# Weights in 4 KB rows with block-diagonal stationaries, and mode-mix groups pinned to iterations, in an attention plus spectral-mix kernel

## The chip, the cores and the metric

The kernel runs on one core of one Trainium2 chip. The metric is device time in microseconds. The kernel before takes 456.05 us, the median of three runs (455.77 to 456.72). A core has a matrix engine (PE; its weight loads are listed apart as PEld), a vector engine (DVE), a scalar engine (ACT), a general engine (POOL), a queue engine (SP), and 16 DMA engines which all of them share.

## The reference

Two stages follow one another. The first is linear attention with a learned feature map, for 8 batches, 8 heads, 576 tokens and head size 64:

```python
proj = einsum('bhsd,df->bhsf', x, w_phi)            # 64 -> 128 features
proj = proj - max(abs(proj), axis=-1, keepdims=True)
phi  = concatenate([exp(proj), exp(-proj)], -1)     # 256 features
kv = einsum('bhsf,bhsd->bhfd', phi(k), v);  z = sum(phi(k), axis=2)
out = einsum('bhsf,bhfd->bhsd', phi(q), kv) / (einsum('bhsf,bhf->bhs', phi(q), z) + 1e-6)
```

The heads side by side make x of 8 x 576 x 512. The second stage mixes it in the frequency domain and adds a channel mix:

```python
X = rfft(x, axis=1)                                  # the first 64 modes are used
Yr = einsum('bmd,mde->bme', Xr, w_r) - einsum('bmd,mde->bme', Xi, w_i)
Yi = einsum('bmd,mde->bme', Xr, w_i) + einsum('bmd,mde->bme', Xi, w_r)
y = irfft(Y, n=576, axis=1)                          # other modes are zero
u = x + y;  result = u + relu(u @ w_ch)
```

Every mode has its own 512 x 512 matrices w_r and w_i in float32. Together they are 134.2 MB, by far the most that the kernel reads; q, k and v are 9.4 MB each, and the result is 9.4 MB.

## The kernel before, in words

**Attention.** 32 items are worked through in a software pipeline of 34 iterations (`for n in range(N + 2)`, L555). Items 0 to 7 are one head for two batches, first head 0 and then head 1 (the first quarter of the 512 channels together, 64 each). Items 8 to 31 are two heads (128 channels, called a quarter g = 1, 2 or 3) of one batch. In iteration n, item n gets its features, item n-1 its products, and item n-2 its forward transform (`x_mm`, L344), which multiplies a token block by a cosine and sine matrix (`CF4`) and leaves the spectrum of 64 modes. `psx` holds it, and ACT copies it into XT0 or XT1. Each engine's order is the order in which the program is written (manual schedule).

**XT.** A tile XT0 or XT1 has a row per channel (128) and 80 columns of 64 modes. Columns 16 to 31 and 48 to 63 hold the spectrum for 8 batches in two parts each; columns 0 to 15, 32 to 47 and 64 to 79 are zero. A stationary of 32 columns that begins at column 0, 16, 32 or 48 puts a mode's 16 rows of result into the upper or the lower half of a 32-row strip, so that two modes share a strip and zeros are added for the other one. XT1 serves head 0 and g = 1 and 3; XT0 serves head 1 and g = 2.

**Mode mix.** The weights come in 32 groups, k = 0 to 31. Groups 0 to 7 are 16 modes for 64 channels each (four DMAs of 1 MB read, the two halves of a tile apart, L167). Groups 8 to 31 are 8 modes for 128 channels: one DMA for w_r and one for w_i (L162), each 2 MB of float32 read and 1 MB of bfloat16 written, as 1,024 rows of 512 numbers (2 KB read, 1 KB written). `mode_mm(k)` multiplies a group (L403, L416), and `mode_sum(k)` adds it to `Yacc` on DVE. The tiles of a group lie in a pool with three buffers (`bufs=3`), so a group k+3 can be loaded once group k has been multiplied.

**What sets the order.** At most one `mode_mm` stands in an iteration, as the last of PE's work there; it runs in the first iteration that is at least `after[k] + 2` and is written up to k = 21. The others follow attention, each with some pieces of the channel mix (`pieces(plan[k])`: transposes of x, their product with w_ch) and every second one with `by_batch`. In an iteration, POOL's order is: loads of q and k (odd n only, `load_qk`, for iterations n+5 and n+6), then `weights(k_in)` while `k_in < k_out + 3`, and then `vscale` (L270, L275), which scales v by the feature factors and whose result `vaug` PE needs for `kv_mm` (L286) one iteration later. All loads that change the type (weights, q, k, w_ch) are issued by POOL on one queue (q0). The built program gives these transfers eight completion counters in turn, so each waits on POOL until the one eight before it has landed, and what stands behind it on POOL waits too. Loads of v and stores go through SP (q1).

Of the kernel before, what the change touches and what calls it, by code (L numbers as in the profile page):

```python
# [21 lines left out]
NCH = 5  # L22
# [4 lines left out]
def kernel(  # L27
# [11 lines left out]
    nc = tc.nc  # L39
# [14 lines left out]
    xs_all = pers.tile([128, B_ * NCH, DMODEL], BF16, name="xs_all")  # L54
# [8 lines left out]
    CF4 = const.tile([128, NCH, 4, 64], BF16, name="CF4")  # L63
# [3 lines left out]
    XTs = [XT0, XT1]  # L67
# [88 lines left out]
    def weights(k):  # L156
        g, gi = groups[k]
        wt = {}
        for ri, w in ((0, moe_w_r), (1, moe_w_i)):
            t = pw.tile([128, 8, DMODEL], BF16, name=f"w{'ri'[ri]}", tag=f"w{ri}")  # L160
            if gi >= 0:
                nc.gpsimd.dma_start(  # L162
                    t, w[8 * gi:8 * gi + 8, g * 128:(g + 1) * 128, :].rearrange("m p e -> p m e"))
            else:
                for x in range(2):
                    mx = 16 * (-1 - gi) + 8 * x
                    nc.gpsimd.dma_start(  # L167
                        t[64 * x:64 * x + 64],
                        w[mx:mx + 8, g * 64:(g + 1) * 64, :].rearrange("m p e -> p m e"))
            wt[ri] = t  # L170
        W[k] = wt
# [172 lines left out]
    def x_mm(st):  # L344
        psx = psum.tile([128, 2, 4, 64], F32, name="psx", tag="tx", bufs=1)
        XT = XTs[st["xt"]][:, 16:80, :].rearrange("p (x y b) m -> p x y b m", x=2, y=4)
        if "bs" in st:

            h = st["h"]
            for i, b in enumerate(st["bs"]):  # L350
                for c in range(NCH):
                    for x in range(2):
                        nc.tensor.matmul(
                            psx[64 * x:64 * x + 64, i, :, :],
                            lhsT=xs_all[:, b * NCH + c, h * 64:(h + 1) * 64],
                            rhs=CF4[:, c, :, :],
                            start=(c == 0), stop=(c == NCH - 1),
                        )
        else:
            g = st["g"]  # L360
            for c in range(NCH):
                nc.tensor.matmul(
                    psx[:, 0, :, :],
                    lhsT=xs_all[:, st["b"] * NCH + c, g * 128:(g + 1) * 128],
                    rhs=CF4[:, c, :, :],
                    start=(c == 0), stop=(c == NCH - 1),
                )
        for i, b in enumerate(st["bs"] if "bs" in st else (st["b"],)):
            nc.scalar.copy(
                XT[:, :, 0:2, b, :],  # L370
                psx[:, i, :, :].rearrange("d (x y) m -> d x y m", x=2),
            )
# [17 lines left out]
    def mode_mm(k, tag="yr"):  # L390
        g, gi = groups[k]
        XT = XTs[1 - g if k < 8 else g % 2]
        wt = W.pop(k)
        if gi < 0:
            psY = psum.tile([128, 2, DMODEL], F32, name="psY2", tag="pC", bufs=1)
            for par in range(2):
                for ri in range(2):
                    for j in range(4):
                        for x in range(2):
                            r = slice(64 * x, 64 * x + 64)  # L400
                            m = 16 * (-1 - gi) + 8 * x + 2 * j + par
                            c0 = (16, 0, 48, 32)[2 * ri + par]
                            nc.tensor.matmul(  # L403
                                psY[32 * j:32 * j + 32, x, :],
                                lhsT=XT[r, c0:c0 + 32, m],
                                rhs=wt[ri][r, 2 * j + par, :],
                                start=(par == 0 and ri == 0), stop=(par == 1 and ri == 1),
                            )
            return psY
        psY = psum.tile([128, DMODEL], F32, name="psY", tag=tag, bufs=1)  # L410
        for ri in range(2):
            for par in range(2):
                for j in range(4):
                    m = 8 * gi + 2 * j + par
                    c0 = (16, 0, 48, 32)[2 * ri + par]
                    nc.tensor.matmul(  # L416
                        psY[32 * j:32 * j + 32, :],
                        lhsT=XT[:, c0:c0 + 32, m],
                        rhs=wt[ri][:, 2 * j + par, :],
                        start=(par == 0 and ri == 0), stop=(par == 1 and ri == 1),  # L420
                    )
        return psY

# [26 lines left out]
    def zeros(i):  # L450
        for z in (0, 32, 64):
            nc.vector.memset(XTs[i][:, z:z + 16, :], 0.0)

    def setup():

# [68 lines left out]

    psY = None
    k_in = k_out = 0
    K_IN_ATTN = 22
    pa_last_cm = None
    with tc.manual_schedule():
        load(S[0], "qk")  # L530
        setup()
        load(S[0], "v")
        load(S[1])
        zeros(1)
        casts(S[0], nc.vector)
        casts(S[1], nc.gpsimd, "q")
        load_qk(1)
        for t in AAs:
            nc.gpsimd.memset(t[:, 0, :, 1152:1216], 1.0)
        for t in e2s:  # L540
            nc.gpsimd.memset(t[64:128, :, NCH - 1:NCH], 1.0)
        casts(S[1], nc.gpsimd, "k")

        pa_first_cm.__exit__(None, None, None)
        pa_last_cm = tc.tile_pool(name="pa_last", bufs=1)
        pa_last = pa_last_cm.__enter__()
        qk2s[2] = qk_pair(pa_last, 2)
        for t in qk2s[2]:
            nc.gpsimd.memset(t[:, :, 9, :], 0.0)
        load_qk(2)  # L550
        weights(0)
        k_in = 1
        transp(S[0], "q")
        transp(S[0], "k")
        for n in range(N + 2):  # L555
            cur = S[n] if n < N else None
            prev = S[n - 1] if 0 <= n - 1 < N else None
            old = S[n - 2] if 0 <= n - 2 < N else None
            nxt = S[n + 1] if n + 1 < N else None
            if n + 2 < N:  # L560
                load(S[n + 2])
            if cur:
                feat_tok(cur, "k", "pB")
                feat_q(cur)
            if psY is not None:
                mode_sum(k_out, psY)
                psY = None
                k_out += 1
            if cur:
                rem_mm(cur)  # L570
                absmax(cur, "k")
                absmax(cur, "rem")
                exps(cur, "q")
            if nxt:
                transp(nxt, "q")
            if prev:
                kv_mm(prev)
                kv_cp(prev)
            if cur:
                ekq(cur, "k")  # L580
            if n < 4:
                vscale(cur)
            if n % 2 == 1 and 5 <= n < N - 5:
                load_qk((n + 5) // 2)
            while k_in < min(k_out + NW, 2 if n < 3 else 32):
                weights(k_in)
                k_in += 1
            if n in (1, 3):
                load_qk((n + 5) // 2)
            if n == 16:  # L590
                nc.gpsimd.dma_start(wchb, moe_w_ch.rearrange("(dc p) e -> p dc e", p=128))
            if cur and n >= 4:
                vscale(cur)
            if nxt:
                transp(nxt, "k")
            if cur:
                exps(cur, "k")
                exps(cur, "rem")
            if prev:
                num_mm(prev, 1)  # L600
                numer(prev, 0)
                num_mm(prev, 0)
                numer(prev, 1)
                numer(prev, 2)
            if old:
                x_mm(old)
            e = n - (N + 2 - N_EARLY)
            if e >= 0:
                sTe = flip_early(e)
            if cur:  # L610
                feat_tok(cur, "q", "pA")
                absmax(cur, "q")
                ekq(cur, "q")
            if n == 0:
                forward_matrix()
            if n == 2:
                zeros(0)
            if 10 <= n < 10 + NCH:
                inverse_matrix(n - 10)
            if e >= 0:  # L620
                times_w_early(e, sTe)
            if k_out < K_IN_ATTN and n >= after[k_out] + 2:
                psY = mode_mm(k_out)
    if psY is not None:
        mode_sum(k_out, psY)
# [157 lines left out]
    u0 = dict(bc=((0, 0), (0, 1)), half=False, late=False, tags=("T2", "T3"))  # L783

    with tc.manual_schedule():
        plan = {22: 3, 23: 3, 24: 2, 25: 2, 26: 2, 27: 1, 28: 2, 29: 1, 30: 1, 31: 0}
        while k_out < 32:
            k = k_out
            gi = groups[k][1]
# [97 lines left out]
```

## Time and profile before

The profiled execution has a span of 456.7 us, against the median of 456.05 us over the three runs and the highest, 456.72 us.

| what | before |
|---|---|
| PE busy, granted clock (mean) | 301.7 us (66%), 0.88 |
| DVE, ACT, POOL busy | 292.0 us, 261.8 us, 198.8 us |
| read from HBM, written to it | 163.64 MB, 9.44 MB |
| weights of groups 8 to 31 | 48 DMAs of 1,024 KB (written side) |
| weights of groups 0 to 7 | 32 DMAs of 512 KB (written side) |

Busy time of an engine says how much of the span it worked; it doesn't say that the engine sets the end. A DMA's size is the written side, so a weight that arrives as bfloat16 counts half of what was read. The DMA share of a queue is the time of its packets over 16 engines' time, and it may be over 100% where packets overlap. The granted clock is that of the matrix engine.

### The profile page before, as it was taken

The page shows a single profiled execution, that of the slowest core. Times are in us where ns is not written, and L with a number is a line of the kernel's source. Part 1 is how long each engine was busy: PE and PEld are TensorE (multiplying, and loading weights), DVE is VectorE, ACT ScalarE, POOL GpSimd, SP SyncE. Part 2 cuts the span into 40 slices and gives each one's busy share as a digit, 9 for nine tenths or more (in the row PEclk, how much of TensorE's full clock was granted, in tenths as well). Part 3 has the DMA queues.
Part 4 walks back from the last instruction along what each step waited for, and adds up shares of the span by engine and source line. Part 5 has one row for each costly group of instructions (what it writes and reads, how often), then busy time and mean ns, then how long its engine had stood idle before and what let it go on. Part 6 is the DMA issues. An engine that isn't in the chain of part 4 may idle for free.

```text
span 456.7 us, 11065 instructions
## 1 busy us (share of the span) xinstructions
PE 301.7 (66%) x4637; PEld 197.6 (43%) x4637; DVE 292.0 (64%) x418; ACT 261.8 (57%) x528; POOL 198.8 (44%) x251
## 2 busy tenths in 40 slices
PE   3476776833767677655555544755578878868993
PEld 2355565622555565544333432433344445433341
DVE  6578789844988779876666472776322273653873
ACT  4576887833686877865545452765334455644662
POOL 3956476445563256553435231443021212100993
PEclk9976899876886769998778595999999999998997
DMA  6999999999999999999999999999999999990697
GB/s 179 195 228 222 225 213 226 221 206 216 221 228 217 230 219 222 224 219 229 218 207 217 218 218 218 207 203 207 207 207 207 207 207 207 207 179 11 223 341 299
DMA packets 84417, 97.70 MB, mean 214 GB/s; under 512 B 3152, under 2 KB 77136, under 8 KB 84368
## 3 DMA queue, kind: packets, MB, share of 16 engines
q0 software_dynamic: 75728, 76.75, 101.1%
q1 hardware_dynamic: 8480, 20.19, 12.8%
q8 instruction: 36, 0.59, 0.5%
q14 instruction: 13, 0.11, 0.1%
q10 hardware_dynamic: 160, 0.07, 0.1%
HBM read 163.64 MB, written 9.44 MB: 379 GB/s over the span
## 4 chain that ended last, share of the span: by engine, by line
DMA 34%; issue 24%; DVE 17%; PE 11%; POOL 7%; ACT 3%; SPq 1%; DVEq 0%; POOLq 0%; ACTq 0%
DMA wi<-in_moe_w_i_dram 29%; DVE mkq L233 6%; DMA wr<-in_moe_w_r_dram 4%; DVE xs_all L336 2%; DVE nd L322 2%; DVE tB L315 2%; POOL vaug L270 2%; PE ptr L184 1%; PE psNB L305 1%; ACT AA L240 1%; PE kvz L286 1%; PE psB L753 1%; DVE of L776 1%; SPq L122 1%; POOL wr L162 1%
## 5 line engine op out<-in xcount | busy, mean ns | idle before, releaser
L270 POOL TENSOR_TENSOR vaug<-vn,ee 128x576 bf16<-128x576 f32 x64 | 72.7, 1155 | 63.3 <-ACT ee L255 50.2
L240 ACT ACTIVATE AA<-psT 128x1024 bf16<-128x1024 f32 x64 | 62.0, 1021 | 43.6 <-PE psT L208 43.1
L262 ACT ACTIVATE e<-mkq 64x4 f32<-64x4 f32 (+1 forms) x128 | 26.3, 206 | 61.5 <-DVE mkq L233 59.2
L244 ACT ACTIVATE AA<-psk 128x1024 bf16<-128x1024 f32 x64 | 61.4, 1010 | 0.0
L162 POOL DMA_DIRECT2D wr<-in_moe_w_r_dram x24 | 21.9, 912 | 86.6 <-PE psY L416 77.8
L416 PEld LDWEIGHTS <-XT 128*32 128x32 bf16 x384 | 17.1, 171 | 56.6 <-issue 46.4
L667 ACT CAST xw<-psW 128x1024 bf16<-128x1024 f32 x17 | 17.2, 1013 | 40.5 <-PE psW L665 34.6
L233 DVE TENSOR_REDUCE mkq<-psk 128x8 f32<-128x1024 f32 x32 | 38.8, 1213 | 0.7 <-PE psk L199 0.7
L233 DVE TENSOR_REDUCE mkq<-psq 128x8 f32<-128x1024 f32 x32 | 38.9, 1217 | 0.4 <-PE psq L199 0.4
L435 DVE TENSOR_TENSOR Yacc<-psY,Yacc 128x512 f32<-128x512 f32 x16 | 11.0, 689 | 42.5 <-PE psY L416 42.5
L416 PE MATMUL psY<-wi,XT 128*32 128x512 bf16 x192 | 18.0, 435 | 28.8 <-DMA wi<-in_moe_w_i_dram 28.8
L286 PE MATMUL kvz<-vaug,AA 64*128 64x65 bf16 x1152 | 29.2, 210 | 11.5 <-POOL vaug L275 9.8
L190 DVE COPY kT<-ptr 128x640 bf16<-128x640 bf16 x32 | 15.7, 492 | 32.5 <-PE ptr L184 32.5
L665 PE MATMUL psW<-wchb,sT 128*128 128x512 bf16 x136 | 33.5, 391 | 2.1 <-ACT xw L667 2.1
L315 DVE TENSOR_TENSOR tB<-psNB,e 128x650 f32<-128x650 f32 x32 | 26.7, 833 | 11.2 <-PE psNB L305 10.6
L305 PEld LDWEIGHTS <-AA 128*128 128x128 bf16 x640 | 29.0, 110 | 9.3 <-issue 8.9
L286 PEld LDWEIGHTS <-AA 64*128 64x128 bf16 x1152 | 25.1, 107 | 15.9 <-issue 11.8
L162 POOL DMA_DIRECT2D wi<-in_moe_w_i_dram x24 | 21.1, 880 | 23.8 <-PE psY L416 20.5
L322 DVE TENSOR_TENSOR nd<-psNA,tB 128x650 f32<-128x650 f32 x32 | 26.7, 835 | 4.1 <-DVE tB L315 0.5
L416 PE MATMUL psY<-wr,XT 128*32 128x512 bf16 x192 | 17.0, 424 | 18.0 <-DMA wr<-in_moe_w_r_dram 8.7
L336 DVE TENSOR_TENSOR xs_all<-nd,rden 128x640 bf16<-128x640 f32 x32 | 28.0, 874 | 1.1
L184 PE MATMUL ptr<-ident_b,k 128*128 128x128 bf16 x160 | 17.9, 257 | 14.8 <-DVE qT L190 12.6
(132 smaller groups left out, 705.4 us busy)
## 6 DMA issues: line engine op xcount, KB each, us to landing
wr<-in_moe_w_r_dram POOLq DMA_DIRECT2D x24, 1024.0 KB, 25.8
wi<-in_moe_w_i_dram POOLq DMA_DIRECT2D x24, 1024.0 KB, 29.4
wr<-in_moe_w_r_dram POOLq DMA_DIRECT2D x16, 512.0 KB, 15.9
wi<-in_moe_w_i_dram POOLq DMA_DIRECT2D x16, 512.0 KB, 19.6
out_dram<-of SPq DMA_DIRECT2D x16, 512.0 KB, 3.8
vn<-in_v_dram SPq DMA_DIRECT2D x24, 288.0 KB, 5.8
q<-in_q_dram POOLq DMA_DIRECT2D x12, 288.0 KB, 19.3
k<-in_k_dram POOLq DMA_DIRECT2D x12, 288.0 KB, 20.0
```

Source lines behind the costliest of these rows:

```text
L162: nc.gpsimd.dma_start(t, w[8 * gi:8 * gi + 8, g * 128:(g + 1) * 128, :].rearrange("m p e -> p m e"))
L233: nc.vector.tensor_reduce(out=o, in_=i, axis=AX.X, op=ALU.max, apply_absolute_value=True)
L240: nc.scalar.activation(AA[:, 0, ab, 0:1024].rearrange("f (x j p) -> f j x p", j=2, p=64), st["psT"].rearrange("f j (x p) -> f j x p", p=64 ...
L244: nc.scalar.activation(AA[:, 1, ab, 0:1024].rearrange("p (c j f) -> p j c f", c=4, j=2), st["psk"], ACT.Exp, scale=sc)
L270: nc.gpsimd.tensor_tensor(out=vaug[:, ab, :, 0:64], in0=st["v"], in1=ee[:, ab, :].unsqueeze(2).to_broadcast([128, 9, D_]), op=ALU.mult,)
L286: nc.tensor.matmul(kvz[:, hh, ab * 65:(ab + 1) * 65], lhsT=AA[r, 1, ab, 128 * j:128 * j + 128], rhs=vaug[r, ab, j, :], start=(j == 0), sto ...
L305: nc.tensor.matmul(p[:, hh, 65 * c:65 * c + 65], lhsT=AA[:, 0, ab, x:x + 128], rhs=kvzF[:, hh, ab * 65:(ab + 1) * 65], start=True, stop=True,)
L315: nc.vector.tensor_tensor(out=tB, in0=st["psNB"], in1=e2.unsqueeze(3).to_broadcast([128, 2, NCH, 65]), op=ALU.mult,)
L322: nc.vector.tensor_tensor(out=nd, in0=st["psNA"], in1=st["tB"], op=ALU.add)
L336: nc.vector.tensor_tensor(out=xo, in0=nd[:, :, :, 0:64], in1=rden.to_broadcast([128, 2, NCH, 64]), op=ALU.mult,)
L416: nc.tensor.matmul(psY[32 * j:32 * j + 32, :], lhsT=XT[:, c0:c0 + 32, m], rhs=wt[ri][:, 2 * j + par, :], start=(par == 0 and ri == 0), sto ...
L665: nc.tensor.matmul(ps[:, x, :], lhsT=sT[:, x, dc, :], rhs=wchb[:, dc, :], start=(dc == 0), stop=(dc == 3))
```

## The change

Four edits belong together.

1. A group with g >= 1 is loaded by four DMAs in place of two. Each takes every second mode (four even or four odd ones) for all 128 channels, and writes 64 partitions: partition p of a half holds channels 2p and 2p+1 of a mode behind one another. A row is then 1,024 numbers (4 KB read, 2 KB written), and a group has 1,024 rows in all instead of 2,048. Bytes and tile sizes are the same.
2. The forward transform of g >= 1 has to give the spectrum in that arrangement: 20 matmuls with 64 stationary columns (every second channel) and 128 moving columns (every second mode) in place of 5 with 128 and 256, and two ACT copies of 64 partitions in place of one of 128. XT then holds even modes in the upper 64 partitions and odd modes in the lower ones, in different columns: the stationary is block-diagonal, and the two modes of a strip are done by one matmul. `mode_mm` keeps 16 matmuls of 128 x 32 by 512, with other columns.
3. Columns of XT1 and XT0 that held spectrum before have to be zero in the lower partitions for the new form: `zeros_late` puts two POOL memsets of 64 x 1,024 into iteration 9 (XT1) and two into iteration 13 (XT0), at the end of the iteration's POOL work. Groups 6 and 7 are multiplied from XT0 in iterations 13 and 14, behind that memset, so in the changed kernel their lower 64 partitions (modes 40 to 47 and 56 to 63 for the channels of head 1) contribute zeros; all their matmuls are still done.
4. The mode mix is written at given iterations (`at`), 19 groups in attention instead of 22, and 13 after it. `plan` now has two pieces per group up to k = 23 and one from there to 30; there are 17 pieces in all, as before.

```diff
@@ weights
-                nc.gpsimd.dma_start(
-                    t, w[8 * gi:8 * gi + 8, g * 128:(g + 1) * 128, :].rearrange("m p e -> p m e"))
+                for y in range(2):
+                    nc.gpsimd.dma_start(
+                        t[64 * y:64 * y + 64].rearrange("p (m i) e -> p m (i e)", i=2),
+                        w[8 * gi + y:8 * gi + 8:2, g * 128:(g + 1) * 128, :].rearrange(
+                            "m (p i) e -> p m (i e)", i=2))
@@ x_mm
-            g = st["g"]
-            for c in range(NCH):
-                nc.tensor.matmul(
-                    psx[:, 0, :, :],
-                    lhsT=xs_all[:, st["b"] * NCH + c, g * 128:(g + 1) * 128],
-                    rhs=CF4[:, c, :, :],
-                    start=(c == 0), stop=(c == NCH - 1),
+            g, b = st["g"], st["b"]
+            for i in range(2):
+                for c in range(NCH):
+                    for y in range(2):
+                        nc.tensor.matmul(
+                            psx[64 * y:64 * y + 64, 0, :, 32 * i:32 * i + 32],
+                            lhsT=xs_all[:, b * NCH + c, g * 128 + i:(g + 1) * 128:2],
+                            rhs=CF4[:, c, :, y::2],
+                            start=(c == 0), stop=(c == NCH - 1),
+                        )
+            for y in range(2):
+                nc.scalar.copy(
+                    XT[64 * y:64 * y + 64, :, 2 * y:2 * y + 2, b, :],
+                    psx[64 * y:64 * y + 64, 0, :, :].rearrange("d (x y) m -> d x y m", x=2),
                 )
-        for i, b in enumerate(st["bs"] if "bs" in st else (st["b"],)):
+            return
+        for i, b in enumerate(st["bs"]):
@@ mode_mm
-            for par in range(2):
+            for i in range(2):
                 for j in range(4):
-                    m = 8 * gi + 2 * j + par
-                    c0 = (16, 0, 48, 32)[2 * ri + par]
                     nc.tensor.matmul(
                         psY[32 * j:32 * j + 32, :],
-                        lhsT=XT[:, c0:c0 + 32, m],
-                        rhs=wt[ri][:, 2 * j + par, :],
-                        start=(par == 0 and ri == 0), stop=(par == 1 and ri == 1),
+                        lhsT=XT[:, 16 + 32 * ri:48 + 32 * ri, 32 * i + 4 * gi + j],
+                        rhs=wt[ri][:, 2 * j + i, :],
+                        start=(i == 0 and ri == 0), stop=(i == 1 and ri == 1),
                     )
@@ new
+    def zeros_late(i):
+        for z in (16, 48):
+            nc.gpsimd.memset(XTs[i][64:128, z:z + 16, :], 0.0)
@@ the loop over iterations
-    K_IN_ATTN = 22
+    at = [5, 6, 7, 8, 9, 11, 13, 14, 17, 18, 20, 21, 23, 25, 27, 28, 30, 31, 33]
...
+            if n in (9, 13):
+                zeros_late(1 if n == 9 else 0)
             if e >= 0:
                 times_w_early(e, sTe)
-            if k_out < K_IN_ATTN and n >= after[k_out] + 2:
+            if k_out < len(at) and n == at[k_out]:
+                assert n >= after[k_out] + 2
                 psY = mode_mm(k_out)
...
-        plan = {22: 3, 23: 3, 24: 2, 25: 2, 26: 2, 27: 1, 28: 2, 29: 1, 30: 1, 31: 0}
+        plan = {k: 2 if k < 24 else int(k < 31) for k in range(k_out, 32)}
```

## The prediction

> **What bounds the kernel now.** I read the page's slices first, then the queues, then the DMA view of two windows, and last the timeline of PE and POOL at the places that the change touches. The slices say which resource never rests.
>
> ```profile
> DMA  6999999999999999999999999999999999990697
> GB/s 179 195 228 222 225 213 226 221 206 216 221 228 217 230 219 222 224 219 229 218 207 217 218 218 218 207 203 207 207 207 207 207 207 207 207 179 11 223 341 299
> ...
> q0 software_dynamic: 75728, 76.75, 101.1%
> ```
>
> The DMA engines are full from the second slice to about 411 us, while PE is at 66% and DVE at 64% of the span. The written side stays between 203 and 230 GB/s whether attention runs or not. So up to the last weights the kernel is a DMA stream, and the other engines matter only where they leave the queue empty. A stretch with weights alone gives the price of a row:
>
> ```profile
> GB/s 206 208 207 207 204 209 207 209 206 206 207 208 208 204 209 214 203 206 207 207 207 207 206 209 214 201 206 208 207 205 207 208 208 205 208 207 206 213 204 206
> DMA packets 10223, 10.36 MB, mean 207 GB/s; under 512 B 159, under 2 KB 10219, under 8 KB 10219
> ## 3 DMA queue, kind: packets, MB, share of 16 engines
> q0 software_dynamic: 10219, 10.30, 123.9%
> ```
>
> This is 340 to 390 us. Of 10,219 packets 159 are completions, so 10,060 rows of 2 KB (read) in 50 us on 16 engines: one per engine every 50,000 x 16 / 10,060 = 79.5 ns, or 412 GB/s read. The end of the stream sets the end of the kernel: the last two groups' matmuls stand on PE as
>
> ```profile
> 404.63 0.69 PE L416 MATMUL psY<-wi,XT 128*32 128x512 bf16 x8 [1.16 <-DMA wi<-in_moe_w_i_dram]
> ...
> 415.56 0.69 PE L416 MATMUL psY<-wr,XT 128*32 128x512 bf16 x8
> ```
>
> Group 30 waits for its weights at 404.63. Group 31 starts at 415.56, where the stream has just ended (the next slice moves 11 GB/s). From there to 456.7 lie 41.1 us of inverse transform and stores, which the change doesn't touch.
>
> **The change part by part.** The sum is made against the span, 456.7 us; the median is 0.65 us lower.
>
> *Rows of 4 KB.* 24 groups x 2,048 rows / 16 engines = 3,072 rows per engine become 1,536. Two rows cost 159.0 ns now. The trace has no cast row of 4 KB, so it is bounded. From above by the stores, whose rows are 4 KB on both sides:
>
> ```profile
> GB/s 200 410 128 0 72 404 312 220 404 225 379 410 379 410 353 202 284 397 412 405 405 410 410 115 218 318 404 410 256 118 404 410 389 415 399 410 246 159 0 0
> ```
>
> Between 425 and 457 us their full slices stand at 410 GB/s, 16 x 4,096 / 410 = 159.8 ns a row: nothing gained, 1,536 x 0.8 = 1.2 us lost. From below by the fastest slice of the weights' window, 214 GB/s written, 428 read: 153.1 ns, and 1,536 x 5.9 = 9.1 us gained. The two ends are close and no row lies nearer to one; I take the middle, 156 ns, a gain of 3.0 ns x 1,536 = 4.6 us. The Trainium skill, DMA: Bandwidth & Descriptors, section Why small descriptors are slow, puts about 3 cycles on each packet beside 32 B per cycle; at its 850 MHz that is 3.5 ns for each row saved, an estimate of 5.4 us in place of 4.6. The trace's 79.5 ns fits its 67 cycles (78.8 ns), but rows of one size can't show the split.
>
> *48 more DMAs.* The first eight groups already come as four DMAs to half the partitions each. From 28 to 38 us, with these, q0 and q1 moved 1.88 and 0.30 MB; from 270 to 280 us, with two DMAs per group, 1.89 and 0.29 MB. That is the same rate within 0.5%, at most 0.05 us per group and 1.2 us over 24, at least nothing. I take 0.4 us. The Trainium skill, on the same page under Rules for kernel authors, speaks against this edit: two transfers to partition halves only serialize, one of 128 partitions should be used, and its fit has about 2.0 us of fixed time per DMA. Paid in full that would be 48 x 2.0 = 96 us, an estimate by that page of the Trainium skill; the two windows contradict it here.
>
> *Attention.* It isn't the bound, so its additions count at nothing as long as the queue has work. Per iteration with g >= 1: PE's transform has 20 matmuls instead of 5. The rows are L362 PE psx x120 at 0.56 us per five and L353 with 20 of 256 columns at 1.28 us (89.88 us, full clock); 128 columns should lie between, so 0 to +0.7 us. The cover is DVE's tB and nd (0.85 us each) while PE has nothing else before psq. Items 0 to 7 carry the larger transform and two copies (2 x 0.39 us) in iterations of 7.9 us, as the chain shows:
>
> ```profile
> 49.63 0.85 DVE tB L315
> ...
> 57.49 0.84 DVE tB L315
> ...
> 144.48 0.85 DVE tB L315
> ...
> 152.35 0.85 DVE tB L315
> ...
> 160.46 0.84 DVE tB L315
> ```
>
> 7.86 us apart at first, and 7.87 and 8.11 us with the smaller one. ACT gets two copies of 64 x 128 in place of 391 ns; each lies between the 205 ns of a tiny exponential and 391 ns, so 0 to +0.4 us, ahead of its wait for DVE's mkq (59.2 us in 32 waits, 1.85 us each). If that cover were gone, up to 24 x 1.1 us would fall on attention. The four memsets: POOL's 128x128 ones take 0.2 us and these have 8 times the elements per partition, so 0.2 to 1.6 us each. At n = 13 they stand between vaug and group 6's matmuls, 0 to 3 us once for PE.
>
> *POOL.* A group with g >= 1 now issues four DMAs of 0.6 to 0.7 us (the 512-row ones take 0.70, q and k with 256 rows 0.73) where two of 0.9 stood: +0.8 us ahead of `vscale`. And it uses four of the eight completion counters, so POOL may look only two groups ahead (20 us) where it looked three. This is what that does in the one stage that has it already:
>
> ```profile
> 89.29 0.69 POOL L167 DMA_DIRECT2D wr<-in_moe_w_r_dram  x1 [1.50 <-DMA wi<-in_moe_w_i_dram]
> 93.13 0.68 POOL L167 DMA_DIRECT2D wr<-in_moe_w_r_dram  x1 [3.15 <-DMA wi<-in_moe_w_i_dram]
> 95.47 0.68 POOL L167 DMA_DIRECT2D wi<-in_moe_w_i_dram  x1 [1.66 <-PE ptr L181]
> 97.76 0.68 POOL L167 DMA_DIRECT2D wi<-in_moe_w_i_dram  x1 [1.61 <-DMA wr<-in_moe_w_r_dram]
> ```
>
> Each issue waits until an old transfer lands, vaug comes late, and PE's kvz waits 6.06 us for it at 100.97. But POOL waits then because eight transfers are queued, so the stream itself stays full; only attention is late.
>
> *The given iterations.* They space the groups so that attention isn't stopped by weights: today psY waits 28.8 us for wi and 8.7 for wr, nearly all in groups 8 to 21. Iteration 17 begins near 163 us; 17 iterations of 7.9 us from there end attention near 297 us instead of 330, with 13 groups behind it at about 10 us each. That moves idle time and not bytes: 0. What counts is whether the queue runs dry. From n = 9 (group 4 multiplied) to n = 33 (group 18) are 24 iterations x 7.9 = 190 us. In that time the queue is given groups 7 to 20, 14 x 10.0 = 140 us, nine pairs of q and k (1.125 x 79.5 ns x 32 x 9 = 26 us), 22 loads of v (16 us) and w_ch (2.5 us): 184 us. With groups 5 and 6 queued at the start (20 us), 14 us are left at the end, so it stays full.
>
> *After attention.* PE did ten groups with all 17 pieces in 84 us; now 13 groups have 115 us, with one piece for each of the last. The last group waits for its weights either way: 0.
>
> Sum: 456.7 - 4.6 + 0.4 = 452.5 us of span, **451.9 us** against the median.
>
> **The rivals.**
>
> A, *the rows are worth nothing*. DMA engines may be bound by bytes. For it: stores of 4 KB move at 410 GB/s, weights of 2 KB at 412. Against it: single slices reach 428. Then 456.05 + 0.4, or 456.5 us, up to 457.
>
> B, *the queue runs dry* (slower). The groups can't move up when attention is late, as they could before. The place is n = 9 to 33: the 14 us of spare are gone when an iteration takes 8.5 us, and each 0.1 us more costs 2.4 us. For it: the iterations around 118 to 137 us took 8.7 to 9.3 us at clock 0.65 to 0.91, POOL's blocked issues made two of 13.7 and 15.0 us, and PE, ACT and POOL each get work. At 8.8 us: 24 x 0.9 - 14 = 7.6 us, giving 459.5 us; with one blocked stretch more it would be 465. Against it: with a clock of 1.0 to 0.7 the iterations kept to 7.9 to 8.1 us, and when POOL is blocked the queue is full by definition.
>
> C, *the rows are worth more than the fastest slice*: if packets of 4 KB overlapped as the present ones do (97 ns busy for one every 79.5), the stream could go below 153 ns, and the time below 446.5 us. Nothing in the trace reads faster than 428 GB/s for a whole slice.
>
> **How the numbers follow.** The forecast, 447 to 455.1 us, gets 0.60; C 0.05; A 0.12; B 0.23. Changes within 0.2% (0.9 us) can't be told from none. Faster is the forecast and C, 0.65; the same is most of A, 0.10; slower is B and the rest of A, 0.25. The forecast alone reaches from 447 (9.1 us of gain) to 455. Leaving out C's lower part and the half of B above 460 gives 446 to 460 us.
>
> **What would show it.** Right: in a window with weights alone, about 5,130 rows of 2 KB (written) in 50 us instead of 10,060 of 1 KB, at 210 GB/s; the DMA row at 9 up to about 406 us; the last group's matmuls near 411 us with the same 41 us behind; iterations of 7.9 to 8.1 us from n = 17 on and few waits of psY for wi; POOL waiting for DMA before its issues without slices under 9. Wrong: 207 GB/s as before (A); digits under 9 in the DMA row between 200 and 320 us, or psY waiting for DMA after attention with a gap in the rate (B).

## The result and the profile after

The changed kernel takes 463.62 us, the median of six runs (461.63 to 466.20), against 456.16 us for the kernel before on the same occasions: a ratio of 1.0152, with a 95% interval from 1.0121 to 1.0182. It is 7.5 us slower, where 4.2 us of gain were forecast, and outside the range. Rival B, the queue running dry, is what happened.

The page of the changed kernel, its slices and its queue. A digit is a fortieth of the span, 11.6 us:

```profile
DMA  6999999999999999999999994999999999991697
GB/s 180 193 230 225 221 211 229 218 209 226 218 231 223 221 231 222 227 227 221 230 223 222 202 183 73 199 167 211 211 211 211 211 211 211 211 211 29 211 342 296
...
q0 software_dynamic: 51920, 76.75, 92.6%
```

Where the kernel before had only nines until its weights ended, there is a 4, and the rate falls to 73 GB/s; the slices around it are low too. The same view for 264 to 304 us, a digit per us:

```profile
DMA  9899999999996100000006999999999989999999
GB/s 201 115 178 201 203 211 221 201 211 211 211 207 121 33 0 0 16 0 0 0 0 111 180 201 205 207 203 209 217 221 203 166 135 201 209 197 219 205 213 211
```

From 277 to 285 us next to nothing moves. The busy times of three stretches (in us, by engine, then the granted clock, the DMA share and, last, the rate in GB/s) give the size of the hole:

```profile
260.00:280.00 20.00, 12.53 (x254) 8.51 (x250) 13.88 (x21) 13.80 (x32) 7.44 (x10) 0.92 0.93 169
280.00:300.00 20.00, 13.22 (x232) 8.19 (x233) 11.90 (x17) 9.42 (x24) 7.48 (x11) 0.83 0.80 144
300.00:320.00 20.00, 14.94 (x130) 7.78 (x130) 4.91 (x8) 5.54 (x8) 6.94 (x12) 0.83 1.01 185
```

Against the 211 GB/s of later stretches that is (42 + 67 + 26) / 211 x 20 = 12.8 us of missing transfers: most of it from 277 to 285 us, the rest in short dips, the largest at 306 to 309 us. The rows themselves did what was forecast. The window with weights alone, 340 to 390 us:

```profile
DMA packets 5451, 10.56 MB, mean 211 GB/s; under 512 B 320, under 2 KB 320, under 8 KB 5447
...
q0 software_dynamic: 5447, 10.50, 111.8%
```

5,447 - 320 = 5,127 rows in 50 us, one per engine every 156.0 ns, against 159.0 for two rows before. The forecast for this window was about 5,130 rows.

The end, on PE:

```profile
418.40 0.68 PE L425 MATMUL psY<-wr,XT 128*32 128x512 bf16 x8
419.98 1.09 PE L425 MATMUL psY<-wi,XT 128*32 128x512 bf16 x8 [0.89 <-DMA wi<-in_moe_w_i_dram]
```

Group 31 is done at 421.1 us; before, it was done at 416.7. What follows takes 42.4 us instead of 40.0, with busy times on DVE, ACT and POOL equal within 0.1 us, and a granted clock of 0.86 instead of 0.94. So of the 6.8 us between the spans, 4.4 lie ahead of the last group and 2.4 behind it.

### The profile page after: what moved, and what is told of

Same layout as the page of the kernel before. It is cut to its first block, busy times and chain, and to the rows that moved or that the text cites. A ratio compares the mean times of both kernels' runs of the same rounds, so it can differ in the third digit from the quotient of the medians.

```text
span 463.5 us, 11860 instructions
## 1 busy us (share of the span) xinstructions
PE 319.8 (69%) x4979; PEld 208.9 (45%) x4997; DVE 293.9 (63%) x418; ACT 270.2 (58%) x552; POOL 220.3 (48%) x303
## 4 chain that ended last, share of the span: by engine, by line
PE 26%; DVE 24%; DMA 21%; ACT 13%; issue 7%; POOL 7%; SPq 1%; DVEq 0%; ACTq 0%; POOLq 0%
DMA wi<-in_moe_w_i_dram 17%; DVE mkq L236 7%; DVE xs_all L339 4%; DVE nd L325 4%; DMA wr<-in_moe_w_r_dram 4%; ACT AA L243 3%; PE psW L681 3%; PE psY L425 3%; DVE tB L318 2%; POOL vaug L273 2%; PE psNB L308 2%; ACT AA L247 2%; PE kvz L289 2%; ACT e L265 2%; PE ptr L187 2%
## 5 line engine op out<-in xcount | busy, mean ns | idle before, releaser
L243 ACT ACTIVATE AA<-psT 128x1024 bf16<-128x1024 f32 x64 | 62.0, 1021 | 11.9 <-PE psT L211 11.3
L163 POOL DMA_DIRECT2D wr<-in_moe_w_r_dram x48 | 30.0, 630 | 69.8 <-PE psY L425 36.8
L163 POOL DMA_DIRECT2D wi<-in_moe_w_i_dram x48 | 29.6, 624 | 54.4 <-DMA wi<-in_moe_w_i_dram 26.2
L681 PE MATMUL psW<-wchb,sT 128*128 128x512 bf16 x127 | 37.0, 430 | 4.0 <-ACT xw L683 2.6
L211 PE MATMUL psT<-qT,w 64*128 64x512 bf16 x64 | 14.5, 441 | 29.1 <-DVE mkq L236 29.0
L308 PEld LDWEIGHTS <-AA 128*128 128x128 bf16 x640 | 30.5, 113 | 7.0 <-issue 6.5
L289 PEld LDWEIGHTS <-AA 64*128 64x128 bf16 x1152 | 25.2, 106 | 16.8 <-issue 12.5
L425 PEld LDWEIGHTS <-XT 128*32 128x32 bf16 x384 | 15.6, 168 | 35.2 <-issue 17.9
L339 DVE TENSOR_TENSOR xs_all<-nd,rden 128x640 bf16<-128x640 f32 x32 | 29.4, 918 | 1.1
L673 DVE COPY sT<-pt 128x1024 bf16<-128x1024 bf16 x17 | 11.8, 691 | 24.0 <-PE pt L670 24.0
```

Of the source, the lines that this page charges most:

```text
L163: nc.gpsimd.dma_start(t[64 * y:64 * y + 64].rearrange("p (m i) e -> p m (i e)", i=2), w[8 * gi + y:8 * gi + 8:2, g * 128:(g + 1) * 128, :] ...
L243: nc.scalar.activation(AA[:, 0, ab, 0:1024].rearrange("f (x j p) -> f j x p", j=2, p=64), st["psT"].rearrange("f j (x p) -> f j x p", p=64 ...
L289: nc.tensor.matmul(kvz[:, hh, ab * 65:(ab + 1) * 65], lhsT=AA[r, 1, ab, 128 * j:128 * j + 128], rhs=vaug[r, ab, j, :], start=(j == 0), sto ...
L308: nc.tensor.matmul(p[:, hh, 65 * c:65 * c + 65], lhsT=AA[:, 0, ab, x:x + 128], rhs=kvzF[:, hh, ab * 65:(ab + 1) * 65], start=True, stop=True,)
L339: nc.vector.tensor_tensor(out=xo, in0=nd[:, :, :, 0:64], in1=rden.to_broadcast([128, 2, NCH, 64]), op=ALU.mult,)
L681: nc.tensor.matmul(ps[:, x, :], lhsT=sT[:, x, dc, :], rhs=wchb[:, dc, :], start=(dc == 0), stop=(dc == 3))
```

## The experiments

Three explanations were tried: D, the pins (and what stands in the pinned iterations) let the queue run dry; H, four DMAs per group hold POOL up at the eight completion counters and make attention late; X, the new transform makes the iterations longer. Two tiles tell the iterations apart: `nd` is written by DVE once in each, and `kvz` is PE's product that needs `vaug`. Code cuts are marked by `...`.

**e1: rows without pins.** The changed kernel with the old rule and the old plan.

```diff
-    at = [5, 6, 7, 8, 9, 11, 13, 14, 17, 18, 20, 21, 23, 25, 27, 28, 30, 31, 33]
+    K_IN_ATTN = 22
...
-            if k_out < len(at) and n == at[k_out]:
-                assert n >= after[k_out] + 2
+            if k_out < K_IN_ATTN and n >= after[k_out] + 2:
...
```

> The changed kernel with the old rule for the mode mix (a group in the first iteration that is at least after[k] + 2, up to group 21) and the old plan; rows of 4 KB, four DMAs per group, the new transform and the memsets stay. Theory D (the pinned iterations let the queue run dry, 11.7 us in the trace of the changed kernel, and the rows themselves gain 1,536 x 3.0 ns): 450 to 453 us, no slice of the DMA row under 9 before 400 us, 211 GB/s written in a window with weights alone. Theory H (four DMAs per group hold POOL up at the eight counters, attention is late, and the queue dries whatever the pins): 456 us or more, with waits of kvz for vaug well over the 10.6 us of the changed kernel.

Measured: 468.60 us, ratio 1.0237 (1.0199 to 1.0274). D alone missed by 16 us. Without the pins the change is worse than with them. POOL and PE around iteration 14 show why:

```profile
139.25 0.63 POOL L163 DMA_DIRECT2D wr<-in_moe_w_r_dram  x1 [2.12 <-DMA wi<-in_moe_w_i_dram]
141.92 0.61 POOL L163 DMA_DIRECT2D wr<-in_moe_w_r_dram  x1 [2.04 <-DMA wi<-in_moe_w_i_dram]
145.44 0.61 POOL L163 DMA_DIRECT2D wi<-in_moe_w_i_dram  x1 [2.90 <-DMA wr<-in_moe_w_r_dram]
147.67 0.61 POOL L163 DMA_DIRECT2D wi<-in_moe_w_i_dram  x1 [1.63 <-DMA wr<-in_moe_w_r_dram]
148.30 2.27 POOL L273 TENSOR_TENSOR vaug<-vn,ee 128x576 bf16<-128x576 f32 x2
```

PE at that time, with its wait in brackets:

```profile
150.82 1.17 PE L289 MATMUL kvz<-vaug,AA 64*128 64x65 bf16 x36 [8.94 <-POOL vaug L278]
```

Every issue waits until an old transfer has landed, vaug comes behind the fourth, and PE waits 8.94 us for it. In all, kvz waits 43.7 us for vaug (before: 9.8). So attention is late at iteration 17, the first that may multiply group 8, and until then nothing beyond group 10 can be loaded. Group 8 starts at 179.90 us (before: 170.72), and the queue has run dry ahead of it. The DMA view of 160 to 200 us:

```profile
DMA  9999999999649999700072799999999999999999
GB/s 246 219 203 210 209 208 270 270 212 189 110 72 200 212 188 173 136 9 0 0 180 115 104 113 170 209 227 201 209 207 235 274 249 208 213 202 213 209 239 278
```

**e2: pins without rows.** The kernel before with `at` and the new plan only.

```diff
-    K_IN_ATTN = 22
+    at = [5, 6, 7, 8, 9, 11, 13, 14, 17, 18, 20, 21, 23, 25, 27, 28, 30, 31, 33]
...
```

> The kernel before with the pinned iterations and the new plan alone: rows of 2 KB, two DMAs per group, the old transform. Theory D: the queue runs dry at groups 16 to 18 (iterations 28 to 33) here too, 5 to 12 us, so 461 to 468 us. Theory X (the pins are fine, and the heavier transform with two ACT copies is what makes iterations 17 to 28 take 8.55 us on average instead of 7.9): iterations return to 7.9 us and the time to within 1 us of 456.

Measured: 459.19 us, ratio 1.0048 (1.0023 to 1.0072), between the two expectations. Pins alone cost 1 to 3 us. From the `nd` of iteration 17 to that of 28 an iteration takes 7.95 us on average here, 8.28 in the changed kernel at the same clock (0.84 and 0.83). Iterations 29 to 31 take 9.6 us each: that is not in the 7.9 that I had used.

**e3: only the split into halves.** The kernel before; rows of 2 KB, but two DMAs of 64 partitions for one of 128.

```diff
-                nc.gpsimd.dma_start(
-                    t, w[8 * gi:8 * gi + 8, g * 128:(g + 1) * 128, :].rearrange("m p e -> p m e"))
+                for y in range(2):
+                    nc.gpsimd.dma_start(
+                        t[64 * y:64 * y + 64],
+                        w[8 * gi:8 * gi + 8, g * 128 + 64 * y:g * 128 + 64 * y + 64, :].rearrange(
+                            "m p e -> p m e"))
```

> The kernel before with each weight DMA of groups 8 to 31 split into two of 64 partitions, rows still 2 KB: 48 more DMAs and four counters per group, nothing else. Theory D: 456 to 457 us (0 to 1.2 us for the additional DMAs, POOL waits only while the queue is full). Theory H: 459 us or more, with slices of the DMA row under 9.

Measured: 467.36 us, ratio 1.0234 (1.0182 to 1.0287). The cost that H expected is there: 48 more DMAs cost 10.7 us under the old rule, with no change to rows, transform or pins. The waits of PE in this run (us in total, times, longest):

```profile
PE kvz L289 <- POOL vaug L278: 45.5, 15, 8.8
```

And in the changed kernel:

```profile
PE kvz L289 <- POOL vaug L278: 10.6, 5, 4.8
```

The pins take most of this wait away (e1, the changed kernel without them, has 43.7 us); that this is because its groups are issued further apart is likely, but wasn't tried by itself. Group 8 starts at 179.78 us here and at 168.16 us in the changed kernel.

The lateness isn't made up later. Group 22, the first after attention, starts at 343.8 us (before: 331.1). PE then takes 84.3 us to group 31 (before: 84.5) and in them doesn't wait for weights; from 340 to 380 us the queue is thin in its turn, 178 and 196 GB/s instead of 207. The last group's weights had landed at 422.7 us, 5.4 us ahead of its first matmul, which shows no wait:

```profile
428.11 0.70 PE L419 MATMUL psY<-wr,XT 128*32 128x512 bf16 x8
```

So in this run it is PE's chain after attention that sets the end, and in e1 too (landed at 420.3, multiplied at 428.6).

**e4: the last pins earlier.** The changed kernel with groups 16 to 20 in iterations 29 to 33, and a plan for eleven groups after it.

```diff
-    at = [5, 6, 7, 8, 9, 11, 13, 14, 17, 18, 20, 21, 23, 25, 27, 28, 30, 31, 33]
+    at = [5, 6, 7, 8, 9, 11, 13, 14, 17, 18, 20, 21, 23, 25, 27, 28, 29, 30, 31, 32, 33]
-        plan = {k: 2 if k < 24 else int(k < 31) for k in range(k_out, 32)}
+        plan = {21: 3, 22: 3, 23: 2, 24: 2, 25: 2, 26: 1, 27: 1, 28: 1, 29: 1, 30: 1, 31: 0}
```

> The changed kernel with the last pins moved forward: groups 16 to 20 in iterations 29 to 33 (before: 16, 17 and 18 in 30, 31 and 33), eleven groups after attention, and a plan of 3, 3, 2, 2, 2, 1, 1, 1, 1, 1, 0 pieces. Theory D: the empty stretch near 276 to 286 us shrinks to under 4 us, and the time is 452 to 456 us. If lateness came from elsewhere (H or X), the time stays at 460 us or more.

Measured: 454.85 us, ratio 0.9948 (0.9915 to 0.9981), and on its page no slice under 9 until the weights end:

```profile
DMA  6999999999999999999999999999999999991697
```

As D expected: pinning the last groups earlier takes 8.8 us off the changed kernel's time. It doesn't show that the pins alone made the hole: e8 gets as much without touching them.

**e5 and e6: vscale ahead of the loads.** e3 and e1, each with vscale first on POOL.

```diff
-            if n < 4:
+            if cur:
                 vscale(cur)
...
-            if cur and n >= 4:
-                vscale(cur)
```

> The kernel of halves only (two DMAs of 64 partitions where one of 128 stood, 2 KB rows, old rule), with one edit: in every iteration vscale stands on POOL ahead of the loads and not behind them. Theory H (POOL, held at the eight counters, brings vaug late, so that attention stalls in iterations of 16 to 17 us, and the queue dries behind it): kvz's waits for vaug fall from 45.5 us to under 15, iterations 14, 24 and 26 lose their 16 to 17 us, and the time returns to 456 to 459 us. If the 48 DMAs cost the time in the queue itself, it stays at 466 us or more.

> The kernel of rows only (rows of 4 KB, four DMAs per group, old rule and plan) with vscale ahead of the loads on POOL. Theory H with the gain of the rows (4.6 us): 451 to 455 us. Without H: 466 us or more.

Measured: 465.97 us for e5 (ratio 1.0214, 1.0157 to 1.0270) and 466.86 us for e6 (1.0231, 1.0193 to 1.0269). H was half right. kvz's wait for vaug falls from 45.5 to 8.0 us in e5, as expected, and iteration 14 from 16.3 to 8.1 us, but only 1.4 us come back, and e6 misses its 451 to 455 us by 12. The hold-up moved. POOL works in its written order, and what stands behind the blocked issues is now late instead: iterations 13 and 15 take 10.2 and 12.1 us, and iteration 11 takes 16.8 us instead of e3's 13.3, because PE waits 8.8 us (e3: 4.7) for another tile of POOL's, `ident_f`. Iterations 24 and 26 still take 15.2 and 15.1 us (e3: 17.0 and 16.6; the kernel before: 14.5 and 15.4), so most of their length isn't due to the halves. And the loads now wait behind vscale: in e5 group 3's are issued at 66.6 us instead of 61.7, and the queue, full there in the kernel before, runs nearly dry from 64 to 67 us. The page of e5 shows both holes:

```profile
DMA  6999989999999997999999999999999999993697
GB/s 178 194 230 223 222 161 215 217 218 218 217 218 217 218 230 139 218 218 217 217 218 218 217 218 218 207 206 207 206 207 206 206 207 206 207 206 55 206 346 299
```

Group 8 starts at 175.66 us, still 5 us late, and group 22 at 338.5, 7.4 us later than in the kernel before; from there PE takes 82.7 us to group 31, with one wait of 0.7 us for weights. So e5's loss is again late attention. H's hold-up is in these traces, but no run takes it away whole, so that it is all of the 10.7 us of e3 isn't shown.

**e7: pins and transform.** e2 with the transform cut into 20 matmuls and two ACT copies, in the old arrangement of XT.

```diff
-                nc.tensor.matmul(
-                    psx[:, 0, :, :],
...
+                        nc.tensor.matmul(
+                            psx[64 * y:64 * y + 64, 0, :, 32 * i:32 * i + 32],
+                            lhsT=xs_all[:, b * NCH + c, g * 128 + 64 * y:g * 128 + 64 * y + 64],
+                            rhs=CF4[:, c, :, 32 * i:32 * i + 32],
```

> The kernel of pins only with the transform cut as in the changed kernel (20 matmuls of 64 x 128 and two ACT copies of 64 partitions) but in the old arrangement of XT, with 2 KB rows and two DMAs per group. Theory X (the transform lengthens iterations 17 to 28 from 7.95 to 8.28 us): 8.2 us or more on average, and the time 2 to 5 us above pins only (459.2). Theory H (the 0.33 us are POOL held at the counters by four DMAs per group): 7.9 to 8.05 us and 459 to 460 us.

Measured: 460.55 us, ratio 1.0086 (1.0054 to 1.0117), 1.4 us above e2. Iterations 17 to 28 take 7.99 us on average, so X falls for these: the transform is covered there, and the 8.28 us come with what e7 lacks, the four DMAs above all, though rows and arrangement of XT differ too. In iterations 29 to 31 the transform isn't covered: 10.3 us on average against 9.6. That is enough to widen the hole: from 260 to 320 us e7 moves 183, 179 and 188 GB/s in 20 us each, e2 199, 200 and 204, or 6.9 and 1.7 us of missing transfers. From the first matmul of group 8 to that of group 16 are 108.7 us in e2, 111.0 in e7 and 114.4 in the changed kernel, so of the 5.7 us by which group 16 is later, 2.3 come with the transform and 3.4 with the rest of the change.

**e8: fewer early blocks.** The changed kernel with `N_EARLY` 2 instead of 6. What I had left out of the sum stands in iterations 28 to 33: six blocks of x go through the channel mix there already (`flip_early`, `times_w_early`).

```diff
-    N_EARLY = 6
+    N_EARLY = 2
...
-        plan = {k: 2 if k < 24 else int(k < 31) for k in range(k_out, 32)}
+        plan = {k: 3 if k < 21 else 2 if k < 24 else int(k < 31) for k in range(k_out, 32)}
```

> The changed kernel with two early channel-mix blocks instead of six (iterations 32 and 33 only) and two more pieces after attention (3, 3, 2, 2, 2, then 1). Theory D (iterations 28 to 31 take 10 us because of the early blocks, so groups 16 and 17 come 4 to 6 us late and the queue is empty that long): iterations 29 to 31 fall to 8 to 8.8 us, the empty stretch near 276 to 286 us shrinks by 4 to 6 us, and the time to 457 to 460 us. If the early blocks don't matter: 462 us or more.

Measured: 454.93 us, ratio 0.9968 (0.9944 to 0.9992), better than D's own 457 to 460. Of the hole 3 us are left: 190, 202 and 208 GB/s from 260 to 320 us. DVE's nd in the changed kernel, in the iterations with early blocks:

```profile
268.15 0.83 DVE L325 TENSOR_TENSOR nd<-psNA,tB 128x650 f32<-128x650 f32 x1
278.02 0.83 DVE L325 TENSOR_TENSOR nd<-psNA,tB 128x650 f32<-128x650 f32 x1
288.54 0.83 DVE L325 TENSOR_TENSOR nd<-psNA,tB 128x650 f32<-128x650 f32 x1
```

The same iterations in e8:

```profile
266.10 0.84 DVE L325 TENSOR_TENSOR nd<-psNA,tB 128x650 f32<-128x650 f32 x1
274.20 0.83 DVE L325 TENSOR_TENSOR nd<-psNA,tB 128x650 f32<-128x650 f32 x1
282.07 0.83 DVE L325 TENSOR_TENSOR nd<-psNA,tB 128x650 f32<-128x650 f32 x1
```

9.9 and 10.5 us become 8.1 and 7.9. The early block adds a chain of its own to each iteration. In the changed kernel's timeline, PE's transposes `pte` wait for ACT's copies into XT, which have to empty the one buffer that `psx` and `pte` share, and the next item's psk waits for ACT to empty the block's product:

```profile
269.91 0.38 PE L389 MATMUL pte<-ident_b,xs_all 128*128 128x128 bf16 x4 [1.77 <-ACT XT L374]
...
273.54 0.40 PE L202 MATMUL psk<-w,kT 64*128 64x128 bf16 x8 [1.69 <-ACT xw L399]
```

Group 16, in iteration 30, is so multiplied at 282.55 us, when the queue has been all but dry for over five us. POOL, which has waited for that, issues the next loads at 283.97:

```profile
282.55 1.10 PE L425 MATMUL psY<-wr,XT 128*32 128x512 bf16 x8
...
283.97 1.28 POOL L163 DMA_DIRECT2D wr<-in_moe_w_r_dram  x2 [4.72 <-PE psY L425]
```

**e9: both repairs.** Pins of e4, two early blocks, the plan 3, 3, 3, 2, 2, 2, then 1, and the memset of XT0 in iteration 15.

```diff
-    N_EARLY = 6
+    N_EARLY = 2
...
-    at = [5, 6, 7, 8, 9, 11, 13, 14, 17, 18, 20, 21, 23, 25, 27, 28, 30, 31, 33]
+    at = [5, 6, 7, 8, 9, 11, 13, 14, 17, 18, 20, 21, 23, 25, 27, 28, 29, 30, 31, 32, 33]
-            if n in (9, 13):
+            if n in (9, 15):
-        plan = {k: 2 if k < 24 else int(k < 31) for k in range(k_out, 32)}
+        plan = {21: 3, 22: 3, 23: 3, 24: 2, 25: 2, 26: 2, 27: 1, 28: 1, 29: 1, 30: 1, 31: 0}
```

> The changed kernel with both repairs and the whole sum: pins of e4 (groups 16 to 20 in iterations 29 to 33), two early blocks as in e8 (plan 3, 3, 3, 2, 2, 2, then 1), and the memset of XT0 in iteration 15, behind groups 6 and 7. Theory D (both repairs remove the same empty stretch of about 9 us): no slice under 9 before 400 us, weights ended by 408 to 410 us, and the time like the better of the two, 452 to 455 us, not the sum of both gains. If they remove different losses: 448 us or less.

Measured: 452.66 us, ratio 0.9906 (0.9874 to 0.9938). This beats both kernels; it is 11.0 us under the changed one and 4.2 under the kernel before. As expected, the two repairs remove one and the same hole: 8.8 and 8.7 us alone, 11.0 together. The 2 us that each lacks alone are near what it leaves of the hole: from 260 to 320 us e4 moves 204, 203 and 203 GB/s, 2.2 us short of 211, e8 is 3.1 us short, and e9 isn't short at all. The DMA view from 264 to 304 us:

```profile
DMA  9999999999999999999999999999999999999999
GB/s 217 205 217 205 211 225 197 217 207 215 207 215 213 215 215 199 217 209 213 209 209 217 213 209 205 219 205 215 211 203 223 199 231 199 213 209 203 223 199 221
```

PE at the end of e9's weights:

```profile
409.54 0.69 PE L425 MATMUL psY<-wi,XT 128*32 128x512 bf16 x8 [1.07 <-DMA wi<-in_moe_w_i_dram]
```

**e10: the same order with 2 KB rows.** The kernel before with the pins, plan and early blocks of e9.

```diff
-    N_EARLY = 6
+    N_EARLY = 2
...
-    K_IN_ATTN = 22
+    at = [5, 6, 7, 8, 9, 11, 13, 14, 17, 18, 20, 21, 23, 25, 27, 28, 29, 30, 31, 32, 33]
-            if k_out < K_IN_ATTN and n >= after[k_out] + 2:
+            if k_out < len(at) and n == at[k_out]:
...
```

> The kernel before with the pins, the plan and the two early blocks of e9, but rows of 2 KB, two DMAs per group and the old transform. What the rows are worth where the queue doesn't run dry is the difference to e9: theory of the price of a row (156.0 ns instead of 2 x 79.5): 4.6 us, less what four DMAs per group cost, so e10 3 to 5 us above e9, at 456 to 459 us. If the gain per row is eaten up by the four DMAs: within 1 us of e9.

Measured: 457.08 us, ratio 0.9998 (0.9973 to 1.0023). Against e9, with a queue that is full in both from 80 us to the last groups, the whole new form (rows of 4 KB, four DMAs, transform, memsets) is worth 457.08 - 452.66 = 4.4 us. With the intervals of the two it is 4 us within 2, which agrees with the 4.6 - 0.4 of the sum but can't tell 0.4 us from nothing.

**e11: the memset of XT0 later.**

```diff
-            if n in (9, 13):
+            if n in (9, 15):
```

> The changed kernel with the memset of XT0 in iteration 15 instead of 13, so that groups 6 and 7 are summed in full. POOL's memsets of 64 x 1,024 stand behind vaug in either place: the same as the changed kernel, 462 to 465 us. If group 6's wait for the memset in iteration 13 mattered: 2 us less.

Measured: 463.12 us, ratio 1.0142 (1.0084 to 1.0200): the same as the changed kernel within the intervals, which are wider than the 2 us of the other expectation. The trace of the changed kernel speaks against it: the memsets hold PE up once, for 0.7 us.

## Why the prediction was wrong

**What bounds the kernel: right for the changed kernel.** There and in e9 the last group's matmuls wait for their weights (0.89 and 1.07 us), and what the changed kernel loses ahead of them is a stretch without transfers. In the kernel before the last group didn't wait: PE came to it 1.6 us after the last row, from a chain of ten groups in 84.5 us that waited for weights once, for 1.2 us. So stream and PE ended there nearly together, and in e1 and e3, where attention is late, it is PE that sets the end.

**Rows of 4 KB: right, and in size.** 156 ns a row was taken, 156.0 measured. The middle between the bounds was luck as far as the trace of before goes. The estimate by the Trainium skill (DMA: Bandwidth & Descriptors, Why small descriptors are slow), 3.5 ns for each row saved, is near the 3.0 ns measured.

**48 more DMAs: right in the queue, wrong on POOL.** In the queue they cost nothing to be seen: e3, with halves, moves 207 GB/s from 372 to 392 us, as the kernels without do. But the step on POOL said that "the stream itself stays full; only attention is late". e3 shows what a late attention does under the old rule: 10.7 us. No group beyond 10 may be loaded until group 8 is multiplied in iteration 17, so the queue dries there, and PE starts its work after attention late. The Trainium skill's advice (DMA: Bandwidth & Descriptors, Rules for kernel authors) to use one transfer for all partitions agrees in its result with e3, though e9, with four DMAs per group, is the fastest of all. The cost isn't paid in the queue, which is where I had tested it with two windows.

**The given iterations: this is the step that failed.** "From n = 9 to n = 33 are 24 iterations x 7.9 = 190 us" was to leave 14 us of spare. Group 4 starts at 93.6 us in the changed kernel and group 18, in iteration 33, at 305.6: 212 us. That is 8.8 us per iteration, and by the sum's own terms 184 us of work and 20 us queued at the start leave the queue empty for 8 us; 12.8 us of transfers were missing. The iterations lengthened in four places. Iterations 10 and 11 took 12.7 and 11.9 us, behind issues that waited at the counters, which the trace of before had shown as 13.7 and 15.0 and which I had named but not added. Iterations 12 to 16 took 8.5 us on average. Iterations 17 to 28 took 8.28 us, where e7, with pins and transform alone, takes 7.99. And 29 to 31 took 9.9 to 10.5, from the early blocks of the channel mix (7.9 to 8.1 without them in e8), which I hadn't read in the loop at all. In the kernel before the same blocks stood in iterations of 9.6 to 10.5 us, where PE waited 0.2 to 1.3 us for weights besides and the queue had work; so the trace held the number, and nothing there showed its price. Rival B had the place and the mechanism, and its 459.5 us at 8.8 us per iteration was 4 us short.

**The sizes.** Rows give 4.6 us and the hole costs 12.8, so 8.2 us net; 4.4 were found at the last group. Part of the rest is that PE came to group 31 1.6 us after its last row in the kernel before, and waits for the DMA in the changed one. Most of what is left lies in the tail of the stream: in its last 14 us, from 400 us on, the kernel before moves 147 GB/s on average, 4.1 us less than at 207, and the changed kernel from 400 to 419.9 us 198 GB/s, 1.2 us less than at 211. Another 2.4 us lie behind the last group, with a lower granted clock; e9, which has the new form too, takes 39.9 us there at a clock of 0.93, so this isn't a cost of the new form. The clock differs between executions of one and the same kernel, too: over the six of the changed kernel its mean lies between 0.839 and 0.885, and the lowest belongs to the one profiled, the second longest. What lowers it wasn't tried.

**The base.** The profiled executions have times of 1.8 to 2.2 us above their span (465.37 for 463.5, 452.34 for 450.1). The sum took 0.65 us off the span for the median instead of comparing spans with spans, a slip that had no part in the sign.

**After attention and the memsets: right; the transform: in part.** PE was in time for the last groups. The transform is covered in iterations 17 to 28 (7.99 us with it, 7.95 without), though not beside the early blocks, where it adds 0.7 us an iteration; the sum had it at nothing as long as the queue has work, and there it ran out. The memsets take 0.95 us each, inside the 0.2 to 1.6 of the bounds, and hold PE up for 0.7 us at most.

## What to carry to other kernels

When a stream of transfers is the bound, a schedule that pins its consumers to iterations must be summed with the length of each iteration, the late ones with their own additional work above all, and not with the typical one. Where the present schedule adapts (a rule "as soon as possible"), waits hide such work, and a fixed schedule takes this cover away. And in this program splitting one transfer into two costs a place in the line of completion counters even where it costs no bandwidth: look at what stands behind the issue on the same engine, and at what the queue may load until that work is done.

## What the runs showed of the hardware

A row of 4 KB read and 2 KB written costs 156.0 ns per engine, and two of half the size 159.0: 211 GB/s against 207 on the written side, in five kernels with the one and four with the other. Splitting the same bytes into two DMAs of 64 partitions leaves 207 GB/s where the queue holds work (e3, 372 to 392 us). I hadn't expected that the granted clock varies so much between executions with nearly the same PE work: behind the last group it was 0.94 in the profiled execution of the kernel before, 0.86 in that of the changed one, and that stretch took 40.0 and 42.4 us.
